# Float32 first tokens on two more queues, 128-token groups, spare PSUM banks for tile 0 and a new order search in a fused attention and MoE kernel

## The chip, the cores and the metric

The kernel runs on one core of a Trainium2 chip. The metric is the device time of one execution in microseconds (us). The profile's span, from the first to the last recorded instruction, is shorter: nearly every run shows 1.8 to 2.0 us between them (313.2 and 311.2 us, for example); two runs of pads0 show 2.8 and 3.2 us. All runs compared are of the state "fast" unless said otherwise.

Engines, as this kernel uses them: PE multiplies matrices, ACT and DVE work on vectors, POOL issues DMA with type conversion, SP issues DMA. Every engine has its own list of instructions, and in the traces here a blocked instruction holds up those behind it: in before, evictions on ACT stand 4.59 us behind an output DMA (shown below).

## The reference, cut to what matters

```python
# q, k, v: [8 batches, 8 heads, 576 tokens, 64], float32
scores = q @ k.T / 8, masked to |i - j| <= 32;  attn = softmax(scores);  o = attn @ v
x = o.transpose(0, 2, 1, 3).reshape(4608, 512)         # tokens x model
h = x @ w_in;  g = max(h, 0)**2;  out = g @ w_out      # w_in 512 x 2048, w_out 2048 x 512
```

## The kernel before

Attention is cut into 72 *steps* of 64 tokens (nine for each batch), the MoE into nine *tiles* of 512 tokens, so tile 0 is steps 0 to 7. For a step, K and Q are turned (transposed) on PE for batches 0 and 1 and by DMA later; then come scores, exp on ACT, mask on DVE, P V on PE, scaling on DVE, and a turn of the result into `XT`. A tile's first layer (`mm1`) reads `XT` and `w_in`; its second (`mm2`) reads `GT` and `w_out`. Tiles 0 and 1 run the first layer in *blocks*: 128 tokens by a quarter of `w_in`, 16 matmuls of 128 columns. Tile 0 has sixteen such blocks, and sixteen second-layer blocks of four matmuls of 512 columns.

```python
ORDER = ("k00 q00 v00 k01 q01 v01 k02 q02 v02 w10 w11 k03 q03 v03 w12 w13 k04 q04 v04 w20 w21 w22 w23 "
         "k10 q10 v10 ...").split()                      # order of the loads on POOL; w1x is w_in, w2x is w_out
PIECE = ((0, 96), (96, 128), (224, 128), (352, 128), (480, 96))    # first token, tokens

# PSUM: 8 banks of 128 x 512 float32
self.SC = ps("sc", [128, 2048], F32)                     # banks A C B D: scores A C, P V on B, turns on D
self.HT = [ps(f"ht{i}", [128, 512], F32) for i in range(2)]      # first layer
self.OUTP = [ps(f"outp{i}", [128, 512], F32) for i in range(2)]  # second layer

m = 1 if b < FB and not c else 2 if b < FB else 3        # steps in a group: 0 | 1 2 | 3 4 | 5 6 | 7 8
...
gt, op = self.GT[T % 2], self.OUTP[x % 2]                # mm2: two output banks
```

The program does not fix the order of the engines' instructions by hand. At build time it records operations with their dependencies, simulates them with assumed durations and DMA landings, and searches for a good order. Where PE has nothing to do in that simulation of the start, it puts *dummy matmuls* on zeros (line 398), which are meant to keep the clock up.

```python
for margin in MARGINS:                                   # 0, 4000, 10000, 20000 ns
    start, T = f[0], f[3]
    for k in range(ROUNDS):                              # 6
        R = self.backward(start, T)
        kk = [... r - (margin if op.att else 0) ...]     # priorities for the next forward pass
        start, end, out, T = self.forward(key=kk)
        keep(out, start, end, T, (margin, k))            # judged under 3 random draws of late DMA
```

The softmax here doesn't subtract the row's maximum and nothing guards it: scores larger than these inputs give would overflow.

## Time and profile before

| what | value |
|---|---|
| time, median of the first runs | 321.35 us (320.57 to 321.36) |
| span of the profiled run, its time | 321.0 us, 322.87 us |
| PE busy | 305.3 us, 95% |
| useful matmul time | 285.9 us |
| lost before 27 us, 27 to 75, 75 to 300, at the end | 18.4, 11.9, 1.6, 3.3 us |

"Useful" and "lost" are my sums and not lines of the profile. I count each real matmul with the spacing at which such matmuls follow each other in the chain of waits (0.216 us for 512 columns, 0.056 for 128, 0.031 for 65, 0.021 for 64) and dummies with zero. Lost time up to a moment is that moment minus the useful time of the matmuls begun by then. The busy share hides this: dummies are busy too.

First, the page of before: span, busy time, and the slices (40 equal parts of the span, in tenths).

```profile
span 321.0 us, 7141 instructions
...
PE 305.3 (95%) x2855; PEld 166.6 (52%) x2855; DVE 151.1 (47%) x448; ACT 148.4 (46%) x263; POOL 107.5 (33%) x133
...
PE   6889989789999998999999999999999999999996
...
DMA  9999999999997999999999999999992221000022
...
L398 PE MATMUL outp<-zz 128*128 128x512 bf16 x51 | 15.6, 409 | 1.2 <-DVE zz L392 1.2
```

PE looks full and DMA is full until about 240 us. But 51 of the matmuls are dummies.

Next, the timeline of PE in before (start, duration, engine, line, operation, result and sources, count, and in brackets the idle time before and what ended it). Lines 623 and 666 are first and second layer, 442 turns of K and Q, 605 turns of step results.

```profile
35.63 1.06 PE L623 MATMUL ht<-xt,w 128*128 128x128 bf16 x16
36.52 5.34 PE L666 MATMUL outp<-w,gt 128*128 128x512 bf16 x24
41.70 0.34 PE L442 MATMUL sc<-identw,kraw 96*128 96x96 bf16 x4
...
42.92 0.40 PE L605 MATMUL sc<-identw,xr 128*128 128x128 bf16 x4 [0.72 <-DVE qt L453]
...
44.50 1.06 PE L623 MATMUL ht<-xt,w 128*128 128x128 bf16 x16
```

Step 7 is paired with step 8, the last of batch 0. Their results are turned only at 42.92 us, behind batch 1's K and Q (41.70). They had been ready for 6.4 us: DVE scaled the second of them from 36.05 to 36.47 us. But the program records the turn of the next group's K and Q first, on the same bank D, so the turn of the results waits until batch 1's K and Q have landed and been copied out. So the ninth first-layer block of tile 0 is at 35.63 us, the tenth only at 44.50.

The timeline of ACT in before shows the stop that follows, and the table of windows what the clock did (columns: window, its length, busy time of PE, PEld (weight loads), DVE, ACT, POOL with counts, granted clock, DMA share, GB/s; the share adds up the packets begun in the window, so it can exceed 1).

```profile
59.96 0.60 ACT L675 ACTIVATE oe<-outp 128x512 f32<-128x512 f32 x1 [0.95 <-PE outp L666]
60.58 4.45 ACTq L677 DMA_DIRECT2D out_dram<-oe  x1
65.14 0.60 ACT L629 ACTIVATE rt<-ht 128x512 bf16<-128x512 f32 x1 [4.59 <-issue]
```

```profile
60.00:65.60 5.60, 2.38 (x51) 2.05 (x48) 0.77 (x3) 1.01 (x2) 1.67 (x2) 1.00 1.80 150
65.60:69.00 3.40, 3.21 (x27) 2.66 (x28) 1.80 (x5) 2.69 (x6) 0.87 (x1) 0.50 1.72 83
```

The first output DMA occupies ACT's queue for 4.45 us. The first-layer results behind it are not evicted, and PE has 2.38 us of work in 5.6 us. Then the clock is granted at half for 3.4 us.

### The profile page before, as it was taken

The numbers are of one execution on the slowest core, as the hardware profiler recorded it, in microseconds if no ns is written. First come the engines' busy times: TensorE is split into PE (matmuls) and PEld (weight loads), VectorE is DVE, ScalarE is ACT, GpSimd is POOL, SyncE is SP. The second block draws the span as 40 slices with busy tenths as digits, with TensorE's granted clock in tenths as the row PEclk, the third lists the DMA queues.
The fourth block names the chain that finished last, engine by engine and source line by source line (L and its number), as shares of the span: only waits on it lengthen the run. The fifth ranks groups of instructions, "written<-read, shape, count | busy, mean of one in ns | idle before, by whom it ended". The sixth has DMA issues, their size and how long they took to land.

```text
span 321.0 us, 7141 instructions
## 1 busy us (share of the span) xinstructions
PE 305.3 (95%) x2855; PEld 166.6 (52%) x2855; DVE 151.1 (47%) x448; ACT 148.4 (46%) x263; POOL 107.5 (33%) x133
## 2 busy tenths in 40 slices
PE   6889989789999998999999999999999999999996
PEld 2455768667755554454454454445444444444442
DVE  5845448445655674454455345545545432222200
ACT  2334436364544665455545545545535544344411
POOL 8999295414302552243333343333320000000000
PEclk9999999979999999999999999999999999999999
DMA  9999999999997999999999999999992221000022
GB/s 63 157 189 194 191 154 155 137 142 150 141 214 77 124 141 192 135 106 158 149 117 121 149 134 158 117 123 140 150 127 59 58 86 39 33 35 33 34 84 82
DMA packets 165922, 38.89 MB, mean 121 GB/s; under 512 B 157184, under 2 KB 161280, under 8 KB 165888
## 3 DMA queue, kind: packets, MB, share of 16 engines
q0 software_dynamic: 116736, 18.36, 86.7%
q1 hardware_dynamic: 43968, 10.63, 23.4%
q10 hardware_dynamic: 5184, 9.44, 9.7%
q8 instruction: 23, 0.38, 0.5%
q14 instruction: 11, 0.09, 0.1%
HBM read 36.70 MB, written 9.44 MB: 144 GB/s over the span
## 4 chain that ended last, share of the span: by engine, by line
PE 80%; DMA 8%; POOL 7%; ACTq 1%; ACT 1%; DVE 1%; issue 1%; SPq 0%; POOLq 0%; DVEq 0%
PE outp L666 37%; PE ht L642 29%; DMA vx<-in_v_dram 6%; PE ht L623 6%; PE sc L529 3%; PE sc L571 2%; PE sc L572 2%; POOL kraw L429 2%; POOL qraw L429 2%; DMA qt<-qraw 2%; POOL vx L478 2%; ACTq L677 1%; POOL w L498 1%; POOL w L493 1%; DVE pt L552 0%
## 5 line engine op out<-in xcount | busy, mean ns | idle before, releaser
L666 PE MATMUL outp<-w,gt 128*128 128x512 bf16 x576 | 143.8, 380 | 0.0
L642 PE MATMUL ht<-xt,w 128*128 128x512 bf16 x448 | 113.9, 379 | 0.0
L648 ACT ACTIVATE rt<-ht 128x512 bf16<-128x512 f32 x112 | 66.7, 599 | 93.2 <-PE ht L642 86.1
L657 DVE TENSOR_TENSOR gt<-rt 128x512 bf16<-128x512 bf16 x144 | 60.3, 422 | 79.7 <-ACT rt L648 68.2
L666 PEld LDWEIGHTS outp<-w,gt 128*128 128x128 bf16 x576 | 53.5, 98 | 58.8 <-issue 0.6
L642 PEld LDWEIGHTS ht<-xt,w 128*128 128x128 bf16 x448 | 41.9, 98 | 46.7
L429 POOL DMA_DIRECT2D kraw<-in_k_dram x40 | 35.3, 882 | 48.1 <-PE ht L642 31.5
L429 POOL DMA_DIRECT2D qraw<-in_q_dram x40 | 35.2, 879 | 43.8 <-PE ht L642 14.6
L478 POOL DMA_DIRECT2D vx<-in_v_dram x40 | 34.9, 873 | 38.2 <-PE sc L572 11.0
L545 ACT ACTIVATE e<-sc 128x512 bf16<-128x512 f32 x72 | 38.2, 601 | 9.5 <-PE sc L529 9.5
L623 PE MATMUL ht<-xt,w 128*128 128x128 bf16 x512 | 33.9, 222 | 4.8 <-ACT rt L629 3.4
L552 DVE TENSOR_TENSOR pt<-e,mask 128x512 bf16<-128x512 bf16 x72 | 26.9, 420 | 18.4 <-ACT e L545 18.2
L623 PEld LDWEIGHTS ht<-xt,w 128*128 128x128 bf16 x512 | 30.2, 99 | 8.5 <-ACT rt L629 4.8
L675 ACT ACTIVATE oe<-outp 128x512 f32<-128x512 f32 x36 | 21.5, 598 | 26.2 <-PE outp L666 26.2
L488 DVE COPY vd<-vx 64x1056 bf16<-64x1056 bf16 (+1 forms) x36 | 17.4, 483 | 28.3 <-DMA vx<-in_v_dram 27.8
L585 DVE TENSOR_TENSOR xr<-sc,rs 128x256 bf16<-128x256 f32 x72 | 29.7, 420 | 1.8
L629 ACT ACTIVATE rt<-ht 128x512 bf16<-128x512 f32 x32 | 19.2, 599 | 24.3 <-PE ht L623 19.5
L583 DVE RECIPROCAL rs<-sc 128x4 f32<-128x4 f32 x72 | 12.8, 180 | 15.4 <-PE sc L572 14.2
L398 PE MATMUL outp<-zz 128*128 128x512 bf16 x51 | 15.6, 409 | 1.2 <-DVE zz L392 1.2
L571 PE MATMUL sc<-vx,pt 128*128 128x65 bf16 x160 | 15.0, 192 | 0.5 <-DVE pt L552 0.3
L572 PE MATMUL sc<-vx,pt 128*128 128x65 bf16 x160 | 15.1, 193 | 0.0
L529 PEld LDWEIGHTS sc<-qt,kt 64*128 64x128 bf16 x576 | 10.0, 95 | 9.8 <-issue 7.9
(38 smaller groups left out, 128.3 us busy)
## 6 DMA issues: line engine op xcount, KB each, us to landing
out_dram<-oe ACTq DMA_DIRECT2D x36, 256.0 KB, 3.3
kraw<-in_k_dram POOLq DMA_DIRECT2D x30, 128.0 KB, 5.1
qraw<-in_q_dram POOLq DMA_DIRECT2D x30, 128.0 KB, 5.9
vx<-in_v_dram POOLq DMA_DIRECT2D x24, 128.0 KB, 5.0
w<-in_moe_w_in_dram POOLq DMA_DIRECT2D x4, 512.0 KB, 10.3
w<-in_moe_w_out_dram POOLq DMA_DIRECT2D x4, 512.0 KB, 17.0
vx<-in_v_dram POOLq DMA_DIRECT2D x16, 96.0 KB, 4.4
kt<-kraw SPq DMA_TRANSPOSE x30, 4.7
```

Of the source, the lines that this page charges most:

```text
L429: self.p.rec("POOL", lambda e: e.dma_start(dst, src), writes=[("fraw", b, t, x)], old=[("fraw", b - 2, t, x)], reads=self.pace(b, x, "kqv" ...
L478: self.p.rec("POOL", lambda e: e.dma_start(self.VX[b % 2][r:r + n, s, :, 0:64], self.v[b, :, t0:t0 + n, :].rearrange("h p d -> p h d")), w ...
L545: self.p.rec("ACT", lambda e, d=dst, a=src: e.activation(d, a, ACTF.Exp, scale=0.125), reads=["s" + x for x in name], writes=[("e", g, x) ...
L552: self.p.rec("DVE", lambda e, a=pt, c=ee, d=mb: e.tensor_tensor(a, c, d, ALU.mult), reads=rd + ["mask"], writes=[("pt", (n + k) % 3)], key ...
L572: mm = e.matmul(o, pt[:, a + 64:a + 192], vt[:, ha + 2, 0:VE], start=False, stop=True)
L585: self.p.rec("DVE", lambda e: e.tensor_tensor(bass.AP(xr, 256 * k, [[768, 128], [64, 4], [1, 64]]), bass.AP(self.SC, base, [[2048, 128], [ ...
L623: mm = e.matmul(ht[:, 128 * (d % 4):128 * (d % 4) + 128], self.W1[:, ft, 128 * d:128 * d + 128], self.XT[:, t0 // 64:t0 // 64 + 2, ft, :], ...
L642: mm = e.matmul(ht[:], self.W1[:, ft, 128 * d:128 * d + 128], self.XT[:, 8 * T:8 * T + 8, ft, :], start=(ft == 0), stop=(ft == 3))
L648: self.p.rec("ACT", lambda e: e.activation(rt[:], ht[:], ACTF.Relu), reads=[("ht", k % 2)], writes=[("rt", k % 4)], key=key, dur=560)
L657: self.p.rec("DVE", lambda e: e.tensor_tensor(g, r, r, ALU.mult), reads=[("rt", k % 4)], writes=tags, key=key, dur=430)
L666: mm = e.matmul(op[:], gt[:, d, 128 * u:128 * u + 128], self.W2[:, d, :], start=(d == 0), stop=(d == 15))
L675: self.p.rec("ACT", lambda e: e.activation(oe[:], op[:], ACTF.Copy), reads=[("outp", x % 2)], writes=[("oe", x % 4)], key=key, dur=560)
```

## The change: its intent and the diff

The change wants PE to start real work earlier and never to wait for batch 1 while work of tile 0 is left. It has five parts: (1) the first 96 tokens of Q, K, V come in float32 through the SP and ACT queues; (2) groups and pieces are aligned to 128 tokens, with 544 tokens early, so that tile 0 needs nothing of step 8; (3) P V of batch 0 alternates between two banks, the turns of its first steps use the first output bank, and the second layer of tile 0 also uses banks B and D; (4) `PACE` is 15 instead of 18, so later loads wait for later work; (5) the search also tries simulations in which every DMA lands later by a fixed amount.

```diff
-PACE = 18
+PACE = 15
-MARGINS, ROUNDS, NREP = (0, 4000, 10000, 20000), 6, 3
+PADS, MARGINS, ROUNDS, NREP = (0, 1000, 2000, 4000), (0, 4000, 10000), 3, 3
-ORDER = ("k00 q00 v00 k01 q01 v01 k02 q02 v02 w10 w11 k03 q03 v03 w12 w13 k04 q04 v04 w20 w21 w22 w23 "
+ORDER = ("k01 q01 v01 k02 q02 v02 w10 k03 q03 v03 w11 w12 k04 q04 v04 w13 w20 w21 w22 w23 k05 q05 "
+TURN0 = {1: 1, 2: 2, 4: 3, 6: 4}
+PIECE0 = ((0, 96), (96, 64), (160, 128), (288, 128), (416, 128), (544, 32))
@@ forward
-  end[op.i] = max(now, start[op.i] + op.dur) + POST[op.eng] + (rnd.random() * rnd.late[op.eng] if rnd else 0)
+  end[op.i] = max(now, start[op.i] + op.dur) + POST[op.eng] + (rnd.random() * rnd.late[op.eng] if rnd else pad)
@@ schedule
+        for pad in PADS:
+            f = self.forward(key=key, pad=pad)
+            for margin in MARGINS:
+                ...
+                    start, end, out, T = self.forward(key=kk, pad=pad)
@@ first loads (float32, no conversion)
+        self.p.rec(eng, lambda e: e.dma_start(dst, src), writes=[("oe", "kqv".index(t))], dma=(f"s{t}", 0), ...)
+                    self.first_load("k", "SP", -300)
+                    self.first_load("q", "ACT", -300)
+                    self.first_load("v", "SP", -299)
@@ banks
-        bank = "ACB"[k] if b >= FB else "B"
+        bank = "ACB"[k] if b >= FB else "BD"[n % 2] if n < 8 else "B"
+        trp, tag = (self.TRP, "sD") if n >= 8 else (self.OUTP[0][:].bitcast(BF16), ("outp", 0))
+        if x in (2, 3):                                  # second layer of tile 0
+            tag = "sB" if x == 2 else "sD"
+            op = self.BK[tag[1]]
@@ groups
-                m = 1 if b < FB and not c else 2 if b < FB else 3
+                m = 3 if b >= FB else 1 if not c or n in (1, 8) else 2
... (float32 turns and copies, keys of the second layer of tile 0, old= bookkeeping)
```

More of the change, by code (lines that the diff above doesn't have):

```diff
@@ L27 @@
 FB = 2
-PACE = 18
+PACE = 15
 ENGS = ("PE", "ACT", "DVE", "POOL", "SP")
-MARGINS, ROUNDS, NREP = (0, 4000, 10000, 20000), 6, 3
+PADS, MARGINS, ROUNDS, NREP = (0, 1000, 2000, 4000), (0, 4000, 10000), 3, 3
 LATE = {"POOL": 1500, "SP": 2000, "ACT": 2000}
 DEPTH, POST, BACK = 4000, {"POOL": 1500, "SP": 1000, "ACT": 1000}, {"POOL": 2500, "SP": 4000, "ACT": 4000}
-ORDER = ("k00 q00 v00 k01 q01 v01 k02 q02 v02 w10 w11 k03 q03 v03 w12 w13 k04 q04 v04 w20 w21 w22 w23 "
+ORDER = ("k01 q01 v01 k02 q02 v02 w10 k03 q03 v03 w11 w12 k04 q04 v04 w13 w20 w21 w22 w23 k05 q05 "
          "k10 q10 v10 k11 q11 v11 k12 q12 v12 k13 q13 v13 k14 q14 v14").split()
+GT0, WT0 = (12.5, 16, 19, 24), (13, 18, 21, 26)
+TURN0 = {1: 1, 2: 2, 4: 3, 6: 4}
+PIECE0 = ((0, 96), (96, 64), (160, 128), (288, 128), (416, 128), (544, 32))
 PIECE = ((0, 96), (96, 128), (224, 128), (352, 128), (480, 96))
@@ L92, in link, with forward @@
                 op.pred.append((d, hard))
-    def forward(self, key=None, seq=None, rnd=None):
+    def forward(self, key=None, seq=None, rnd=None, pad=0):
         ops = self.ops
@@ L282, in keep @@
                 best = (s, out, start, end, T)
-        f = self.forward(key=key)
-        keep(f[2], f[0], f[1], f[3], "keys")
-        for margin in MARGINS:
-            start, T = f[0], f[3]
-            for k in range(ROUNDS):
-                R = self.backward(start, T)
-                kk = [1e4 * op.key if op.key <= -100 else r - (margin if op.att else 0) for r, op in zip(R, self.ops)]
-                start, end, out, T = self.forward(key=kk)
-                keep(out, start, end, T, (margin, k))
+        for pad in PADS:
+            f = self.forward(key=key, pad=pad)
+            keep(f[2], f[0], f[1], f[3], ("keys", pad))
+            for margin in MARGINS:
+                start, T = f[0], f[3]
+                for k in range(ROUNDS):
+                    R = self.backward(start, T)
+                    kk = [1e4 * op.key if op.key <= -100 else r - (margin if op.att else 0) for r, op in zip(R, self.ops)]
+                    start, end, out, T = self.forward(key=kk, pad=pad)
+                    keep(out, start, end, T, (pad, margin, k))
         self.log, self.R = log, R
-        s, out, start, end, T = best
+        out = best[1]
+        start, end, out, T = self.forward(seq={e: [o for o in out if o.eng == e] for e in ENGS})
         for op in self.ops:
@@ L388, in alloc @@
         self.OE = [sb(f"oe{i}", [128, 512], F32) for i in range(4)]
+        self.STG = dict(zip("kqv", self.OE))
+        self.IDF = self.OE[3][:, 0:128]
     def ms(self, eng, t, ap, v, key, dur=120, old=()):
@@ L402, in setup_masks @@
                    key=key, dur=400)
+        self.p.rec("DVE", lambda e: e.tensor_scalar(self.IDF, self.IOTA[:, 0:128], 0.0, None, ALU.is_equal),
+                   reads=["iota"], writes=[("oe", 3)], key=key - 0.1, dur=200)
         self.p.rec("DVE", lambda e: e.tensor_scalar(self.IDW[:], self.IOTA[:], 64.0, None, ALU.is_equal),
@@ L423, in setup_ptz, with pieces, slot, first_load @@
             self.ms("DVE", [("ptz", i)], self.PT[i][:, 192 * j + 64:192 * j + 128], 0.0, key, 70)
+    def pieces(self, b):
+        return PIECE2 if b >= FB else PIECE if b else PIECE0
+    def slot(self, b, x):
+        return 512 * (x if b else x - 1)
+    def first_load(self, t, eng, key):
+        src = (self.q if t == "q" else self.k if t == "k" else self.v)[0, :, 0:96, :].rearrange("h p d -> p h d")
+        r = 32 if t == "v" else 0
+        dst = bass.AP(self.STG[t], 512 * r, [[512, 96], [64, 8], [1, 64]])
+        self.p.rec(eng, lambda e: e.dma_start(dst, src), writes=[("oe", "kqv".index(t))], dma=(f"s{t}", 0), key=key, dur=400,
+                   move=(48, 14))
@@ L425, in tok_load, with first_v @@
+    def first_v(self, key):
+        for r, n in ((32, 32), (64, 64)):
+            src = bass.AP(self.STG["v"], 512 * r, [[512, n], [64, 8], [1, 64]])
+            self.p.rec("ACT", lambda e, r=r, n=n, c=src: e.activation(self.VX[0][r:r + n, 0, :, 0:64], c, ACTF.Copy),
+                       reads=[("oe", 2)], writes=[("vxl", 0, 0) if r == 32 else ("vxl", 0, 0, 1)], key=key, dur=560, att=True)
     def tok_load(self, b, t, x, key):
-        t0, n = (PIECE if b < FB else PIECE2)[x]
+        t0, n = self.pieces(b)[x]
@@ L427, in tok_load @@
         src = (self.q if t == "q" else self.k)[b, :, t0:t0 + n, :].rearrange("h p d -> p h d")
-        dst = bass.AP(self.RAW[t][b % 2], 512 * x, [[2560, n], [64, 8], [1, 64]])
-        self.p.rec("POOL", lambda e: e.dma_start(dst, src), writes=[("fraw", b, t, x)], old=[("fraw", b - 2, t, x)],
-                   reads=self.pace(b, x, "kqv".index(t)), dma=(f"f{b % 2}{t}{x}", b), key=key,
+        dst = bass.AP(self.RAW[t][b % 2], self.slot(b, x), [[2560, n], [64, 8], [1, 64]])
+        y = x - 1 if not b else x
@@ L431, in tok_load @@
+        self.p.rec("POOL", lambda e: e.dma_start(dst, src), writes=[("fraw", b, t, x)], old=[("fraw", b - 2, t, y + (b == 2))],
+                   reads=self.pace(b, x, "kqv".index(t)), dma=(f"f{b % 2}{t}{y}", b), key=key,
                    dur=500 + 3.2 * n, move=(n // 2, 13.3))
     def tok_turn(self, b, x, key):
-        t0, n = PIECE[x]
+        t0, n = self.pieces(b)[x]
         early = b == 0 and x < 3
-        parts = [("k", ("ht", 0), self.HT[0][:].bitcast(BF16)), ("q", ("ht", 1), self.HT[1][:].bitcast(BF16))] if early else [
-            ("k", "sD", self.TRP[:, 0:512]), ("q", "sD", self.TRP[:, 512:1024])]
+        first = b == 0 and x == 0
@@ L439, in f @@
+        if early:
+            parts = [(t, ("ht", u), self.HT[u][:] if first else self.HT[u][:].bitcast(BF16)) for u, t in enumerate("kq")]
+        elif b or x == 5:
+            parts = [("k", "sD", self.TRP[:, 0:512]), ("q", "sD", self.TRP[:, 512:1024])]
+        else:
+            o = self.OUTP[0][:].bitcast(BF16)
+            parts = [("k", ("outp", 0), o[:, 0:512]), ("q", ("outp", 0), o[:, 512:1024])]
         def f(e, todo):
@@ L441, in f @@
                 for j in range(4):
-                    mm = e.transpose(ps[:, 128 * j:128 * j + n],
-                                     bass.AP(self.RAW[t][b % 2], 512 * x + 128 * j, [[2560, n], [1, 128]]),
-                                     self.ID[0:n, 0:n])
+                    src = bass.AP(self.STG[t], 128 * j, [[512, n], [1, 128]]) if first else bass.AP(
+                        self.RAW[t][b % 2], self.slot(b, x) + 128 * j, [[2560, n], [1, 128]])
+                    mm = e.transpose(ps[:, 128 * j:128 * j + n], src, self.IDF[0:n, 0:n] if first else self.ID[0:n, 0:n])
             return mm
         for todo in ([parts[:1], parts[1:]] if early else [parts]):
-            self.p.rec("PE", lambda e, a=todo: f(e, a), reads=[("fraw", b, t, x) for t, _, _ in todo] + ["id"],
-                       writes=list({tag for _, tag, _ in todo}), key=key, dur=240 * len(todo), att=True)
+            rd = [("oe", "kq".index(t)) for t, _, _ in todo] + [("oe", 3)] if first else [("fraw", b, t, x) for t, _, _ in todo]
+            self.p.rec("PE", lambda e, a=todo: f(e, a), reads=rd + ["id"],
+                       writes=list({tag for _, tag, _ in todo}), key=key, dur=700 if first else 240 * len(todo), att=True)
         for t, tag, ps in parts:
@@ L452, in tok_turn @@
             dst = self.KT[b % 2][:, :, 32 + t0:32 + t0 + n] if t == "k" else self.QT[b % 2][:, :, t0:t0 + n]
-            self.p.rec("DVE", lambda e, d=dst, c=src: e.tensor_copy(d, c), reads=[tag], writes=[(t, b % 2, x)],
-                       old=self.was(b, t, x), key=key, dur=400, att=True)
+            if early and t == "q":
+                self.p.rec("ACT", lambda e, d=dst, c=src: e.activation(d, c, ACTF.Copy), reads=[tag], writes=[(t, b % 2, x)],
+                           old=self.was(b, t, x), key=key, dur=200 + 2.8 * n, att=True)
+            else:
+                self.p.rec("DVE", lambda e, d=dst, c=src: e.tensor_copy(d, c), reads=[tag], writes=[(t, b % 2, x)],
+                           old=self.was(b, t, x), key=key, dur=60 + 3.2 * n, att=True)
     def pace(self, b, x, z):
@@ L464, in was @@
             return []
-        return [(t, b % 2, y) for y in range(5)]
+        return [(t, b % 2, y) for y in range(6)]
     def dma_turn(self, b, t, x, key):
@@ L479, in vx_load @@
             self.VX[b % 2][r:r + n, s, :, 0:64], self.v[b, :, t0:t0 + n, :].rearrange("h p d -> p h d")),
-            writes=[("vxl", b % 2, s)], reads=self.pace(b, s, 2), dma=(f"vf{b % 2}{s}", b), key=key, dur=500 + 3.2 * n, move=(n // 2, 13.3))
+            writes=[("vxl", b % 2, s), ("vxl", b % 2, s, 1)], reads=self.pace(b, s, 2), dma=(f"vf{b % 2}{s}", b), key=key, dur=500 + 3.2 * n, move=(n // 2, 13.3))
     def vd_half(self, b, s0, s1, key):
@@ L486, in vd_half @@
             src = vx[64 - 64 * lo:128 - 64 * lo, s0 + lo:s1 + lo, :, :].rearrange("p s h d -> p (s h d)")
-            rd = [("vxl", b % 2, s + lo) for s in range(s0, s1)] + [("vxone", b % 2, k) for k in range(4)]
+            rd = [("vxl", b % 2, s + lo) + u for s in range(s0, s1) for u in ((), (1,))] + [("vxone", b % 2, k) for k in range(4)]
             self.p.rec("DVE", lambda e, d=dst, c=src: e.tensor_copy(d, c), reads=rd,
@@ L504, in qk_tags @@
         rd = [("ktpad", i, 0), ("ktpad", i, 1)]
-        for x, (t0, n) in enumerate(PIECE if b < FB else PIECE2):
+        for x, (t0, n) in enumerate(self.pieces(b)):
             if t0 < 64 * c + 96:
@@ L575, in av @@
         if c % 2 == 0:
-            rd = [("vxl", i, s)] + [("vxone", i, k) for k in range(4)]
+            rd = [("vxl", i, s), ("vxl", i, s, 1)] + [("vxone", i, k) for k in range(4)]
             if s in (0, 4):
@@ L604, in f @@
                     o = 256 * u + 128 * t
-                    mm = e.transpose(self.TRP[:, o:o + 128], xr[:, u, 128 * t:128 * t + 128], self.ID)
+                    mm = e.transpose(trp[:, o:o + 128], xr[:, u, 128 * t:128 * t + 128], self.ID)
             return mm
-        self.p.rec("PE", f, reads=[("xr", gi % 3, u) for u in range(m)] + ["id"], writes=["sD"], key=key, dur=112 * m, att=True)
-        src = self.TRP[:, 0:256 * m].rearrange("p (n f q) -> p n f q", n=m, f=4)
+        self.p.rec("PE", f, reads=[("xr", gi % 3, u) for u in range(m)] + ["id"], writes=[tag], key=key, dur=112 * m, att=True)
+        src = trp[:, 0:256 * m].rearrange("p (n f q) -> p n f q", n=m, f=4)
         self.p.rec("ACT", lambda e: e.activation(self.XT[:, n:n + m], src, ACTF.Copy),
-                   reads=["sD"], writes=[("xt", n + u) for u in range(m)], key=key, dur=200 + 180 * m, att=True)
+                   reads=[tag], writes=[("xt", n + u) for u in range(m)], key=key, dur=200 + 180 * m, att=True)
     def mm1_small(self, T, g, q, key):
@@ L661, in mm2 @@
         x = 4 * T + u
-        gt, op = self.GT[T % 2], self.OUTP[x % 2]
+        gt, op, tag = self.GT[T % 2], self.OUTP[x % 2][:], ("outp", x % 2)
+        if x in (2, 3):
+            tag = "sB" if x == 2 else "sD"
+            op = self.BK[tag[1]]
         def f(e):
             for d in range(4 * seg, 4 * seg + 4):
-                mm = e.matmul(op[:], gt[:, d, 128 * u:128 * u + 128], self.W2[:, d, :], start=(d == 0), stop=(d == 15))
+                mm = e.matmul(op, gt[:, d, 128 * u:128 * u + 128], self.W2[:, d, :], start=(d == 0), stop=(d == 15))
             return mm
         self.p.rec("PE", f, reads=[("gt", T % 2, d, u) for d in range(4 * seg, 4 * seg + 4)] + [("w2", seg)],
-                   writes=[("outp", x % 2)], key=key, dur=854)
+                   writes=[tag], key=key, dur=854)
         if x == 1 and seg == 0:
@@ L674, in mm2 @@
             oe = self.OE[x % 4]
-            self.p.rec("ACT", lambda e: e.activation(oe[:], op[:], ACTF.Copy), reads=[("outp", x % 2)],
+            self.p.rec("ACT", lambda e: e.activation(oe[:], op, ACTF.Copy), reads=[tag],
                        writes=[("oe", x % 4)], key=key, dur=560)
@@ L681, in moe @@
         if T == 0:
-            gt = (12.0, 15.5, 19.0, 22.0)
-            wt = (13.0, 18.0, 22.0, 28.0)
-            for g, q in sorted(((g, q) for g in range(4) for q in range(4)), key=lambda a: (max(gt[a[0]], wt[a[1]]), a)):
-                self.mm1_small(0, g, q, 0.0 + 0.01 * self.k1)
+            for g, q in sorted(((g, q) for g in range(4) for q in range(4)), key=lambda a: (max(GT0[a[0]], WT0[a[1]]), a)):
+                self.mm1_small(0, g, q, 0.01 * self.k1)
+            for seg in range(4):
+                for u in range(4):
+                    self.mm2(0, u, seg, 0.5 + seg + 0.1 * u)
             return
@@ L692, in moe @@
                 self.mm1(T, d, key)
-            self.mm2(T - 1, d // 4, d % 4, key + 0.25)
+            if T > 1:
+                self.mm2(T - 1, d // 4, d % 4, key + 0.25)
     def build(self):
@@ L701, in build @@
         self.setup_idle()
-        self.setup_masks(K + 2.5)
+        self.setup_masks(K - 20)
         self.setup_rest(0, K + 3)
@@ L718, in build @@
             if b < FB:
-                for bb in range(FB if not b else 0):
-                    for x in range(5):
-                        for t in "kq":
-                            self.tok_load(bb, t, x, at[f"{t}{bb}{x}"])
-                        self.vx_load(bb, x, at[f"v{bb}{x}"])
+                if not b:
+                    self.first_load("k", "SP", -300)
+                    self.first_load("q", "ACT", -300)
+                    self.first_load("v", "SP", -299)
+                    self.first_v(-LEAD - 2.5)
+                for bb in range(0 if b else FB):
+                    for x in range(6):
+                        for t in "kqv":
+                            if f"{t}{bb}{x}" not in at:
+                                continue
+                            if t == "v":
+                                self.vx_load(bb, x, at[f"v{bb}{x}"])
+                            else:
+                                self.tok_load(bb, t, x, at[f"{t}{bb}{x}"])
             else:
@@ L736, in build @@
                         self.tok_turn(0, 0, -LEAD - 3)
+                    if n == 8:
+                        self.moe(0)
+                        tile = 1
+                        self.tok_turn(0, 5, -LEAD + 5)
                     self.scores(n, m)
@@ L739, in build @@
                         bb, cc = divmod(n + m, NCH)
-                        self.tok_turn(bb, (cc + 1) // 2, n + m - LEAD - 3)
+                        if n + m != 8:
+                            self.tok_turn(bb, (cc + 1) // 2 if bb else TURN0[cc], n + m - LEAD - 3)
+                if c and not b:
                     x = (c + 1) // 2
-                    if x and not b:
+                    if c % 2:
                         self.vd_half(b, x - 1, x, n - LEAD - 3)
```

## The prediction

> **What bounds the kernel now.** PE, 95% busy on the page; the chain of waits is 80% PE. But the first slices hold dummy matmuls (51 on zeros) and waits. I add up useful matmuls at their spacing in the chain (four of 512 columns 0.86 us, sixteen of 128 columns 0.89 us; dummies zero). Useful work is about 286 us of the 321.0 us span, so 35 us are lost: 19 before 27 us, 11 from 27 to 75 us, 1.5 from there to 300 us, 3 at the end. Only the start-up can shrink; PE work hardly changes.
>
> **Start-up, from DMA landings and the PE timeline.** Transfers land one after the other: 128 tokens of one tensor each 0.83 us, a weight quarter each 2.6 us; w_in quarters at 16.8, 19.5, 24.5, 27.1 us, w_out at 31.5 to 40.4, batch 1 complete at 51.7 us. The first K lands at 4.4 us: POOL starts issuing at 1.3 us, 0.9 us each. Steps 6 and 7 are turned in pairs (5,6), (7,8); step 7 only at 42.9 us, behind batch 1's K and Q. So PE has done nine of tile 0's sixteen first-layer blocks at 36.5 us, does six second-layer blocks, waits for batch 1, and finishes the sixteen near 53 us; ten second-layer blocks remain after 58 us. At 60.6 us the first output DMA holds the ACT queue 4.45 us, PE stops 3.4 us behind it, and the granted clock is 0.79 from 64 to 72 us.
>
> **What the change does.**
> - Three pieces of 96 tokens leave POOL (2.5 us of issue) for the SP and ACT queues. They must stay float32: the Trainium skill, "DMA: Bandwidth & Descriptors", section "SWDGE vs HWDGE vs iDMA", says only the software queue casts; in the trace POOL issues all casting loads. Float32 turns and ACT copies cost about 3 us on idle engines. The bytes stay; the stream comes 1.5 to 2.5 us earlier (estimate).
> - Groups aligned to 128 tokens, 544 tokens loaded early: steps 6,7 are ready near 28 us, not 43. The sixteen blocks end near 33 us instead of 53.
> - Two more output banks and separate keys: sixteen second-layer blocks (13.8 us) fit into 33 to 48 us, while batch 1 lands. Tile 1 follows without a gap.
> - A smaller PACE holds later loads back by six first-layer blocks, partly cancelling the earlier PE.
>
> **Sum.** Lost before 27 us: 13.4 instead of 19 (nine blocks of 0.89 us and seven steps of attention are useful by then). From 27 to 75 us: 3 to 5 instead of 11. Ideal about 306 us. I give back 4 us: DMA engines read 9 tenths up to 240 us, and from 113 to 124 us PE already waits on a Q transpose; PE 12 us earlier meets batches 2 to 4 with less lead. The early outputs also issue from ACT while DMA is full.
>
> **Predicted: 310.5 us, range 303.5 to 318.5; faster by over 2% 0.78, within 2% 0.20, slower 0.02.**
>
> **What the profile would show.** Right: first K turned by 4.4 us; w_in's first quarter landed near 14 us; tile 0's first layer done before 35 us, its second by 50 us; clock 1.0 from 60 to 75 us; batch 1 complete near 49.5 us; 22 us lost by 75 us instead of 30. Wrong: a step of tile 0 turned after 35 us, PE gaps over 1 us from 30 to 75 us, ACT queue issues over 2 us.
>
> **What would make it wrong.** The instruction orders come from a simulated schedule; a wrong landing in it stops in-order PE. Three queues share the same engines, so the float32 pieces could delay POOL's. Batches 2 and 3 may come too late, giving back up to 8 us near 80 to 125 us.

## The result, and the profile after

After takes 313.18 us (median of 4 runs, 312.09 to 313.32); before took 320.96 us in the same rounds. The ratio is 0.9754, 95% interval 0.9722 to 0.9787. Ratios here and below are the mean time of one kernel's fast runs over that of the other's of the same rounds, so they are not quite the ratio of the medians that I quote. A second set, on another chip, gave 0.9751.

The lines of the page of after that answer to those of before:

```profile
span 311.2 us, 7131 instructions
...
PE 302.4 (97%) x2850; PEld 166.0 (53%) x2850; DVE 147.3 (47%) x448; ACT 151.5 (49%) x269; POOL 105.8 (34%) x132
...
PE   5999999999999999999999999999999999999996
...
DMA  9999999999979999999899999999999220000021
```

The dummies are down to 38. The timeline of PE in after (line 665 first layer, 711 second layer, 479 turns of K and Q, 647 turns of step results):

```profile
22.00 1.07 PE L665 MATMUL ht<-xt,w 128*128 128x128 bf16 x16
22.91 0.81 PE L405 MATMUL outp<-zz 128*128 128x512 bf16 x3
23.56 0.39 PE L479 MATMUL outp<-identw,kraw 128*128 128x128 bf16 x4
...
25.53 0.40 PE L647 MATMUL outp<-identw,xr 128*128 128x128 bf16 x4 [0.29 <-DVE qt L493]
...
26.62 1.96 PE L665 MATMUL ht<-xt,w 128*128 128x128 bf16 x32
...
31.55 0.39 PE L647 MATMUL outp<-identw,xr 128*128 128x128 bf16 x4
...
40.65 1.06 PE L665 MATMUL ht<-xt,w 128*128 128x128 bf16 x16
41.54 2.75 PE L711 MATMUL sc<-w,gt 128*128 128x512 bf16 x12
```

Steps 6 and 7 are turned at 31.55 us, 11 us earlier than step 7 was. The sixteenth first-layer block starts at 40.65 us, and second-layer work on the spare banks (`sc<-w,gt`) fills the rest. The ACT timeline and the windows of after show the stop gone:

```profile
42.60 0.60 ACT L720 ACTIVATE oe<-sc 128x512 f32<-128x512 f32 x1 [0.27 <-PE sc L711]
43.23 0.36 ACTq L722 DMA_DIRECT2D out_dram<-oe  x1
```

```profile
60.00:65.60 5.60, 4.83 (x72) 3.88 (x72) 3.55 (x13) 1.79 (x3) 1.23 (x2) 1.00 1.80 175
65.60:69.00 3.40, 3.40 (x65) 2.89 (x63) 2.11 (x7) 3.10 (x6) 1.58 (x3) 1.00 1.38 194
```

Landings of loads, read from the trace, in us:

| load | before | after |
|---|---|---|
| first K | 4.39 | 4.14 |
| w_in quarters | 16.81, 19.53, 24.45, 27.05 | 12.64, 19.23, 21.25, 26.14 |
| last w_out quarter | 40.40 | 36.30 |
| batch 1 complete | 51.70 | 48.95 |

Lost time as defined above, by part of the run, in us:

| | to 27 us | 27 to 75 | 75 to 300 | end | all |
|---|---|---|---|---|---|
| before | 18.4 | 11.9 | 1.6 | 3.3 | 35.1 |
| after | 17.7 | 1.8 | 2.7 | 3.2 | 25.4 |
| predicted for after | 13.4 | 3 to 5 | about 5.5 | 3 | about 26 |

Nearly all of the gain comes from 27 to 75 us. The profiled run of before was 1.5 us slower than the median of its other runs, so the spans differ by 9.8 us and the times by 7.8.

### The profile page after: what moved, and what is told of

Same layout as the page of the kernel before. It is cut to its first block, busy times and chain, and to the rows that moved or that the text cites. A ratio compares the mean times of both kernels' runs of the same rounds, so it can differ in the third digit from the quotient of the medians.

```text
span 311.2 us, 7131 instructions
## 1 busy us (share of the span) xinstructions
PE 302.4 (97%) x2850; PEld 166.0 (53%) x2850; DVE 147.3 (47%) x448; ACT 151.5 (49%) x269; POOL 105.8 (34%) x132
## 4 chain that ended last, share of the span: by engine, by line
PE 82%; DMA 12%; issue 2%; DVE 1%; ACT 1%; POOL 1%; SPq 0%; POOLq 0%; ACTq 0%
PE outp L711 33%; PE ht L684 27%; PE ht L665 8%; DMA vx<-in_v_dram 7%; PE sc L569 3%; PE sc L611 3%; PE sc L612 2%; PE outp L405 2%; DMA kraw<-in_k_dram 2%; DMA kt<-kraw 2%; DMA oe<-in_v_dram 1%; PE sc L711 1%; DVE vd L528 1%; PE outp L647 0%; POOL qraw L458 0%
## 5 line engine op out<-in xcount | busy, mean ns | idle before, releaser
L711 PE MATMUL outp<-w,gt 128*128 128x512 bf16 x544 | 132.3, 379 | 0.0
L684 PE MATMUL ht<-xt,w 128*128 128x512 bf16 x448 | 109.6, 379 | 0.0
L711 PEld LDWEIGHTS outp<-w,gt 128*128 128x128 bf16 x544 | 51.1, 98 | 57.8
L684 PEld LDWEIGHTS ht<-xt,w 128*128 128x128 bf16 x448 | 42.0, 98 | 47.7 <-ACT rt L690 0.5
L458 POOL DMA_DIRECT2D qraw<-in_q_dram x40 | 33.8, 846 | 48.3 <-PE ht L684 21.8
L458 POOL DMA_DIRECT2D kraw<-in_k_dram x40 | 33.9, 848 | 46.0 <-PE ht L684 21.7
L518 POOL DMA_DIRECT2D vx<-in_v_dram x39 | 33.2, 852 | 34.1 <-PE ht L684 25.5
L720 ACT ACTIVATE oe<-outp 128x512 f32<-128x512 f32 x34 | 20.4, 599 | 27.2 <-PE outp L711 27.2
L665 PE MATMUL ht<-xt,w 128*128 128x128 bf16 x512 | 31.9, 219 | 0.2
L665 PEld LDWEIGHTS ht<-xt,w 128*128 128x128 bf16 x512 | 29.1, 98 | 2.2 <-ACT xt L652 0.7
L569 PE MATMUL sc<-qt,kt 64*128 64x64 bf16 x576 | 13.7, 192 | 0.5 <-ACT qt L490 0.3
## 6 DMA issues: line engine op xcount, KB each, us to landing
w<-in_moe_w_out_dram POOLq DMA_DIRECT2D x4, 512.0 KB, 16.7
```

The costliest lines, as they stand in the source:

```text
L458: self.p.rec("POOL", lambda e: e.dma_start(dst, src), writes=[("fraw", b, t, x)], old=[("fraw", b - 2, t, y + (b == 2))], reads=self.pace( ...
L518: self.p.rec("POOL", lambda e: e.dma_start(self.VX[b % 2][r:r + n, s, :, 0:64], self.v[b, :, t0:t0 + n, :].rearrange("h p d -> p h d")), w ...
L569: mm = e.matmul(sc[:, o + 64 * j:o + 64 * j + 64], kt[r, j, at:at + 128], qt[r, j, at:at + 64], start=True, stop=True)
L665: mm = e.matmul(ht[:, 128 * (d % 4):128 * (d % 4) + 128], self.W1[:, ft, 128 * d:128 * d + 128], self.XT[:, t0 // 64:t0 // 64 + 2, ft, :], ...
L684: mm = e.matmul(ht[:], self.W1[:, ft, 128 * d:128 * d + 128], self.XT[:, 8 * T:8 * T + 8, ft, :], start=(ft == 0), stop=(ft == 3))
L711: mm = e.matmul(op, gt[:, d, 128 * u:128 * u + 128], self.W2[:, d, :], start=(d == 0), stop=(d == 15))
```

## The experiments

**Theory A:** the gain is made of several parts, each worth some us: the earlier load stream, the groups, the spare banks. **Rival B:** the earlier stream alone is the cause. **Rival C:** the new order search alone is the cause. Each run below undoes one part of after, or puts one part alone on before. Such an edit also makes the search find another order for the whole program, so what a run differs by is that part *with* the order found for it. An order alone can move the time of the same program by 1.5 us (pad3000 against after) or 10 us (pads0), so a difference of 3 or 4 us is put down to a part only as far as the trace shows where it arises.

| run | edit | median us | ratio to before (95%) |
|---|---|---|---|
| after | | 313.18 | 0.9754 (0.9722 to 0.9787) |
| after_again | none, another chip | 312.9 | 0.9751 (0.9726 to 0.9776) |
| before_again | none | 321.79 | 1.001 (0.9963 to 1.0057) |
| pool_first | after, first tokens by POOL | 317.0 | 0.9873 (0.9818 to 0.9927) |
| groups_old | after, groups of before | 317.13 | 0.9878 (0.9822 to 0.9934) |
| mm2_two | after, two output banks | 316.48 | 0.986 (0.979 to 0.993) |
| pv_b | after, P V and result turns as before | 316.38 | 0.9847 (0.9825 to 0.9868) |
| turn_ht | after, K and Q turns on other banks | 315.46 | 0.9825 (0.9788 to 0.9863) |
| pads0 | after, search of before | 323.24 (322.81 without a slow run) | 1.0045 (1.0009 to 1.0081) |
| b_search | before, search of after | 321.11 | 1.0007 (0.9958 to 1.0057) |
| pace18 | after, PACE 18 | 314.17 | 0.9775 (0.9723 to 0.9827) |
| pad3000 | after, search with 3 us alone | 311.64 | 0.9702 (0.9666 to 0.9739) |
| turn4_d_3000 | pad3000 and one turn on bank D | 314.28 | 0.975 (0.9711 to 0.9788) |

Nine of the traces from these rounds (before_again, after_again, pool_first, groups_old, mm2_two, turn_ht, pads0, turn4_d_3000 and pv_b) lack 1 to 2% of the matmul records; the eight kernels of the after family among them have 2,796 to 2,818 of about 2,850. A missing record would count as lost time, so for these I give lost time only up to 50 us, and read later parts from waits and clock.

### before_again (no edit)

> The kernel before, unchanged, profiled once more: a control. Theory: the first profile of before (time 322.87 us, span 321.0) caught an exceptional stop of the ACT queue (4.45 us at its first output, PE stopped 3.4 us behind it, clock halved for 3.4 us); the timed runs of before lie 1.5 us lower. So here: time near 321, span near 319.2, no ACT queue issue over 2 us, mean granted clock 1.0. Rival: the stop is regular, and shows again with about the same length. Ratio to before 1.000 either way.

Measured: time 322.56 us in the profiled run, span 320.7. The ACT queue is held again, for 4.23 us at 60.19 us, and the clock is halved for 6.8 us from 64.0 us. My theory falls and the rival holds: the stop is regular. All but one of the eleven runs of before in these rounds have mean granted clocks of 0.988 to 0.995; one or two stretches of 3.4 us at half clock give that. The gap between span and time, 1.8 to 2.0 us, is there in every run of this round.

### pool_first

```diff
-ORDER = ("k01 q01 ...
+ORDER = ("k00 q00 v00 k01 q01 ...
-        first = b == 0 and x == 0
+        first = False                    # bf16 pieces by POOL; the float32 loads are taken out
```

> The kernel after, but the first 96 tokens of Q, K, V are loaded by POOL with the cast to bfloat16, as before; groups, banks and search stay. Theory A (the groups and the banks carry most of the gain, the earlier stream 2 to 3 us): 315 to 316 us, first-layer weights landing 1.5 to 3 us later than in after. Rival B (the earlier stream carries nearly all of it): 319 us or more. Rival C (the float32 path gives nothing, since DMA is saturated from the start): 313 us.

Measured: 317.0 us, ratio 0.9873. The w_in quarters land at 15.52, 21.82, 24.03 and 28.90 us (after: 12.64, 19.23, 21.25, 26.14) and batch 1 is complete at 51.73 us instead of 48.95. Lost time at 27 us is 18.6 us instead of 17.7, at 50 us 21.0 instead of 18.1. So the earlier stream is worth 2.6 to 2.9 us of landing and about 0.012 of the ratio, a little more than theory A said. Rival C's reading (nothing) is refuted. Rival B's (nearly all) does not fit the median, though the interval just reaches its 319 us (0.991).

### groups_old

```diff
-PIECE0 = ((0, 96), (96, 64), (160, 128), (288, 128), (416, 128), (544, 32))
+PIECE0 = ((0, 96), (96, 128), (224, 128), (352, 128), (480, 96))
-                m = 3 if b >= FB else 1 if not c or n in (1, 8) else 2
+                m = 3 if b >= FB else 1 if not c else 2
                 # and the turns, moe(0) and k05 q05 as before
```

> The kernel after, but with the step groups, token pieces and turn order of before (pairs 1-2, 3-4, 5-6, 7-8; no 544-token piece); float32 start, banks and search stay. Theory A: step 7 is turned only behind batch 1's keys, the sixteen first-layer blocks of tile 0 end after 45 us again, and the time goes back to 316 to 319 us. Rival B (the earlier stream is the cause): within 1 us of after, 312 to 314 us.

Measured: 317.13 us, ratio 0.9878. The sixteenth first-layer block of tile 0 starts at 47.9 us (after: 40.65). Up to 30 us this run has lost even less than after (16.7 against 17.7 us), but 5.7 us more are lost from there to 50 us, against 0.4 in after. As theory A said: the old pairs cost their time between 30 and 50 us, waiting for batch 1. The timeline of PE shows the waits (line 611 is P V of step 7, on bank D behind batch 1's K and Q; line 647 the turn of its result):

```profile
37.37 0.33 PE L479 MATMUL sc<-identw,kraw 96*128 96x96 bf16 x4 [0.96 <-DMA qraw<-in_q_dram]
...
38.59 0.20 PE L611 MATMUL sc<-vd,pt 128*128 128x65 bf16 x1 [0.72 <-DVE qt L493]
...
39.74 0.40 PE L647 MATMUL outp<-identw,xr 128*128 128x128 bf16 x4 [0.52 <-DVE xr L625]
40.83 8.08 PE L665 MATMUL ht<-xt,w 128*128 128x128 bf16 x112 [0.69 <-ACT xt L652]
```

The four stops are 2.9 us together, and the clock is halved for 3.4 us from 41.2 us, which is up to 1.7 us more.

### mm2_two

```diff
-        if x in (2, 3):
+        if False:
-            for seg in range(4):
-                for u in range(4):
+            for u in range(4):
+                for seg in range(4):      # two banks: a row block must be closed before the next opens
```

> The kernel after, but the second layer of tile 0 uses the two output banks alone (row blocks one after the other instead of four at once); all else stays. Theory A: second-layer blocks of tile 0 must wait for whole row blocks of the first layer and for evictions, so a part of the gain goes: 314.5 to 317 us. Rival (banks do not matter, since PE always finds other work in 27 to 60 us): within 1 us of after.

Measured: 316.48 us (315.35 to 319.53, a wide spread), ratio 0.986. By 50 us PE has begun ten second-layer blocks instead of twelve (counted by their weight loads, since matmul records are missing), and one wait of 2.8 us for a scaled step result follows, with the clock halved for 3.4 us from 61.0 us:

```profile
61.72 0.61 PE L647 MATMUL sc<-identw,xr 128*128 128x128 bf16 x4 [2.77 <-DVE xr L625]
```

The time is in the size theory A gave. That the two banks cause this wait, and not the order found with them, is not shown.

The three parts together (0.012, 0.012 and 0.011 of the ratio) are more than the whole gain of 0.025. They are not independent: each removes stops, and a stop also costs clock. The mean granted clock shows it: 0.988 to 0.995 in all four runs of groups_old and 0.989 to 0.995 in three of the four of mm2_two, as in before, against 0.998 to 1.0 in after and 0.999 to 1.0 in pool_first.

### after_again, pads0 and b_search: the search

After_again is a control on the chip of pads0.

> The kernel after, unchanged: a control on this chip beside the other variants. Ratio to before 0.974 to 0.977, so 312.5 to 314.5 us if before is near 321.5; all times 1.8 to 2.0 us above their spans, as in every run so far.

Measured: 312.9 us, ratio 0.9751, as expected.

```diff
# pads0: after, with the search of before
-PADS, MARGINS, ROUNDS, NREP = (0, 1000, 2000, 4000), (0, 4000, 10000), 3, 3
+PADS, MARGINS, ROUNDS, NREP = (0,), (0, 4000, 10000, 20000), 6, 3
```

> The kernel after with the schedule search of before (no added DMA delay in the search; four margins, six rounds). If the new search is a cause of its own (a rival to groups, banks and stream), the time goes back by 2 us or more, 315 us and up; if not, within 1 us of after.

Measured: 323.24 us with one slow run, 322.81 us without, ratio 1.0045: *the whole gain is gone*. (Two of the runs have an unusually large gap of 2.8 and 3.2 us between span and time; by spans alone, 319.8 to 320.5 us, there is still no gain.) Up to 50 us the run is like after_again (both have lost about 18.9 us). The loss comes later. The waits of PE in pads0 from 75 to 300 us (total, times, longest), and the longest of them in its timeline:

```profile
PE sc L569 <- DMA qt<-qraw: 4.2, 4, 2.7
PE ht L684 <- DMA xt<-xr: 2.2, 2, 1.7
```

```profile
158.72 0.54 PE L569 MATMUL sc<-qt,kt 64*128 64x64 bf16 x24 [2.73 <-DMA qt<-qraw]
```

PE stands in front of scores whose turned Q has not landed, although further down its list stands work that then starts without a wait of its own (a first-layer block at 159.18 us). The clock is halved for 3.4 us from 159.1 us. In the windows from 100 to 200 us PE is busy 46.10 and 46.29 of 50 us each in pads0, against 49.83 and 49.44 in after, and 49.37 and 49.53 in after_again, whose trace lacks as many records. In after, the waits listed for PE from 20 to 300 us hold only 0.2 us for DMA.

```diff
# b_search: before, with nothing of the change but the search
-MARGINS, ROUNDS, NREP = (0, 4000, 10000, 20000), 6, 3
+PADS, MARGINS, ROUNDS, NREP = (0, 1000, 2000, 4000), (0, 4000, 10000), 3, 3
                 # forward(pad=...) and the loop over PADS as in the diff of the change
```

> The kernel before with nothing of the change but the new search of the instruction orders (each candidate also searched with 0, 1, 2 or 4 us added to every DMA landing). Theory (the search and the shorter start-up only pay together: the search removes stops that appear when PE runs ahead of DMA, and before has hardly any, 1.5 us from 75 to 300 us): 319 to 322 us, ratio 0.992 to 1.003. Rival (the search is the gain by itself, and start-up adds nothing, as the run without it, 323.2 us, could also be read): 313 to 315 us.

Measured: 321.11 us, ratio 1.0007. The search alone gives nothing. So the new start without the new search is worth nothing, the new search without the new start is worth nothing, and both together are worth 2.5%. The margins and rounds of pads0 include those of after, so what its search lacks is the added delay. One order was built for each search, so how much of the 10 us is the delay and how much the luck of that one order is not separated. Rival C falls as "alone" and stays as "necessary".

### pv_b and turn_ht: the shared bank

In after the turn of steps 4 and 5 (25.53 us above) uses the same bank as the last full turn of K and Q (23.56 us), and waits for its copies, although the scaled result was ready at 23.0 us.

```diff
# pv_b: P V of batch 0 on B alone, turns of results on D
-        bank = "ACB"[k] if b >= FB else "BD"[n % 2] if n < 8 else "B"
+        bank = "ACB"[k] if b >= FB else "B"
-        trp, tag = (self.TRP, "sD") if n >= 8 else (self.OUTP[0][:].bitcast(BF16), ("outp", 0))
+        trp, tag = (self.TRP, "sD")
```

> The kernel after, but P V of batch 0 on bank B alone and the turns of its results on bank D, as before; the turns of K and Q stay on the first output bank. Theory: in after the turn of steps 4,5 waits 2.5 us (ready at 23.0, run at 25.5 us) because it shares the bank with the turn of the last K and Q piece; with banks of their own it runs by 23.5 us and one to three first-layer blocks move before 26 us: 0 to 2 us faster than after, 311 to 314 us. Rival (the second P V bank is what matters): P V of a pair is serialized by its scaling, and the time is 0.5 to 2 us longer than after.

Measured: 316.38 us, ratio 0.9847. The time is on the rival's side and longer than it said. The profiled run fell in a slow state (523.75 us at a granted clock of 0.566), so its trace cannot say why; the four fast runs agree within 0.3 us.

```diff
# turn_ht: pieces 3 and 4 of K and Q are turned on the first-layer banks
-        early = b == 0 and x < 3
+        early = b == 0 and x < 5
```

> The kernel after, but pieces 3 and 4 of K and Q are turned on the two first-layer banks, as pieces 0 to 2 are, so that the turn of steps 4,5 shares no bank with them. Theory: the turn of steps 4,5 comes earlier, but first-layer blocks wait for these banks instead; within 1.5 us of after, either way. Rival (the shared bank costs all of the 3.6 us that I missed before 27 us): 310.5 us or less.

Measured: 315.46 us, ratio 0.9825. First-layer work is pushed back as feared: the first block starts at 23.4 us (after: 14.4), and lost time at 27 us is 18.5 us. The cost is larger than the 1.5 us expected.

### pace18

```diff
-PACE = 15
+PACE = 18
```

> The kernel after with PACE 18 again: loads of batches 2 on may go out six first-layer blocks earlier. My prediction's term: the smaller PACE holds loads back and gives a little of the gain back. Then earlier loads help in 80 to 130 us: 311.5 to 313 us. Rival (early loads of batch 2 crowd the start-up, where DMA is full, so batch 1 or the weights land later): 314 to 317 us, with batch 1 complete later than 49.5 us.

Measured: 314.17 us, ratio 0.9775. The interval overlaps nearly all of that of after, so PACE decides nothing that I can see. The time lies in the rival's range, but its mark does not show: batch 1 is complete at 48.37 us, not later than 49.5. My prediction's term, that the smaller PACE gives a part of the gain back, is not supported.

### pad3000

```diff
-PADS, MARGINS, ROUNDS, NREP = (0, 1000, 2000, 4000), (0, 4000, 10000), 3, 3
+PADS, MARGINS, ROUNDS, NREP = (3000,), (0, 4000, 10000), 3, 3
```

> The kernel after with the search run at one added DMA delay of 3 us (after's order came from the candidate with 2 us). Theory: in-order waits on late DMA are what is left between 75 and 300 us (2.7 us in after, 10 us and more in the run without added delay), so more reserve removes 0.5 to 2 us: 311 to 313 us, no PE wait on DMA after 75 us. Rival (2 us is enough, and more reserve displaces other work): 313 to 316 us.

Measured: 311.64 us (310.91 to 312.84, 6 runs), ratio 0.9702. It beats before clearly and has the lowest time and profiled span (309.8 us) of all runs. Against after's two sets its interval overlaps (0.9666 to 0.9739 against 0.9726 to 0.9776), so that it beats after is likely, not shown. Its trace is complete: 1.1 us are lost from 75 to 300 us instead of 2.7, the start to 50 us is as in after, and no wait of PE for DMA is left after 20 us. That is the theory's half of the expectation.

### turn4_d_3000

```diff
# pad3000, and:
-        elif b or x == 5:
+        elif b or x >= 4:                 # piece 4 of K and Q is turned on bank D ...
-                        if n + m != 8:
+                        if n + m not in (6, 8):
                 self.av(n)
+                if n == 5:                # ... recorded after P V of step 5
+                    self.tok_turn(0, 4, 6 - LEAD - 3)
```

> The run with 3 us of added delay (0.970 of before), and one thing more: the last full piece of K and Q is turned on bank D, recorded after P V of step 5, so that the turn of steps 4,5 neither shares its bank nor waits behind it. Theory (this shared bank explains most of the 3.6 us by which I overrated the gain before 27 us): the turn of steps 4,5 runs by 23.7 us instead of 25.5, lost PE time at 30 us falls from 17.6 to under 16 us, and the time is 0.5 to 2 us lower, 309.5 to 311 us. Rival (as the two earlier runs with other banks suggest, blocks moved forward are paid back by steps 6,7, whose turn on D waits longer, and by bank D being taken): lost time at 30 us over 17, time 312 to 315 us.

Measured: 314.28 us, ratio 0.975. Its timeline of PE:

```profile
22.82 1.07 PE L665 MATMUL ht<-xt,w 128*128 128x128 bf16 x16
23.73 0.39 PE L647 MATMUL outp<-identw,xr 128*128 128x128 bf16 x4
...
93.07 0.20 PE L611 MATMUL sc<-vx,pt 128*128 128x65 bf16 x1 [1.73 <-DVE pt L592]
...
95.14 0.82 PE L569 MATMUL sc<-qt,kt 64*128 64x64 bf16 x24 [0.98 <-DVE xr L625]
```

The turn of steps 4 and 5 does move, from 25.51 us in pad3000 to 23.73. It saves little: lost time at 27 us is 16.6 instead of 17.6 us, at 30 us 17.0 instead of 17.6. So neither expectation holds whole: 17.0 lies above the theory's 16, and the time is the rival's. What the new order costs comes later. At 93 us PE stops twice, 2.7 us together, and the windows around it show what the clock made of that:

```profile
84.00:91.00 7.00, 6.84 (x85) 3.58 (x86) 3.65 (x12) 2.08 (x5) 0.00 (x0) 1.00 0.59 127
91.00:94.40 3.40, 1.43 (x48) 1.11 (x40) 1.73 (x8) 2.05 (x4) 0.00 (x0) 0.98 0.52 135
94.40:101.20 6.80, 6.06 (x44) 2.89 (x45) 3.23 (x10) 2.77 (x5) 1.75 (x2) 0.51 0.46 51
101.20:108.00 6.80, 6.75 (x46) 3.24 (x45) 3.50 (x10) 3.77 (x7) 3.98 (x5) 1.00 1.32 98
```

Half a clock over 6.8 us is another 3.4 us at most, on top of 2.7. The runs of this kernel with a full clock (313.48 and 313.82 us) are still 2 us slower than pad3000; where these 2 us go is open, since the trace lacks records.

## Why the prediction was right or wrong, point by point

The time was within the range (310.5 predicted, 303.5 to 318.5; measured 313.2), and faster by over 2% was the likely side. The mechanism was right where the gain arose, from 27 to 75 us. That the sum of the losses came so near (26 us predicted, 25.4 measured) is partly luck: 4.3 us too little before 27 us were balanced by about 2 us too much from 27 to 75 us and about 3 us too much after that.

- **Time against span: wrong by 1.9 us.** I worked from the span of one profiled run (321.0 us) and set its result beside a time (321.35 us) as if they were one thing. They only looked alike because that run was itself 1.5 us slow: its time was 322.87 us. Its own terms also add up to more than I wrote: 321.0 minus 5.6 minus about 7 is 308, not "ideal about 306"; with 4 given back, 312 us of span. Measured: 311.2.
- **"Lost before 27 us: 13.4 instead of 19": the step that was mis-sized most.** Measured 17.7 in after, against 18.4. I took nine first-layer blocks to be done by then; four were begun before 26.6 us (14.41, two at 19.37, 22.00). I had counted a step as ready a few us after its data landed. In fact the last V piece of steps 4 and 5 landed at 15.19 us and the results were turned at 25.53. In turn4_d_3000, without the shared bank (and with another order), the turn comes 1.8 us earlier and 1.1 us less is lost at 27 us; I take the rest to be the chain of scores, exp, mask, P V and scaling on engines in order, which I did not take apart. I also overlooked the clock of the first microseconds. Its record begins, at full, only at 11.62 us in after (4.18 in before, 9.38 in before_again), and the page's PEclk row shows nothing of this; but dummies of 512 columns follow each other at about twice the distance until then:

```profile
7.43 1.89 PE L405 MATMUL outp<-zz 128*128 128x512 bf16 x4
...
13.54 1.02 PE L405 MATMUL outp<-zz 128*128 128x512 bf16 x4
```

By my spacings 1.7 us of useful work in after was begun before 11.62 us (in before none before 4.18), so up to 1.7 us (my estimate) of the 4.3 us that I missed may be the clock.

- **"From 27 to 75 us: 3 to 5 instead of 11": the direction right, and the gain larger.** Measured 1.8 instead of 11.9. Groups_old, mm2_two and pool_first each lose a part of it. The finer claims failed: the first layer of tile 0 ended near 41.5 us and not before 35, and the second at about 60 us (the fourth output eviction of tile 0 is at 60.05 us) and not by 50. It did not matter, since PE had first-layer blocks of tile 1 in between.
- **"The stream comes 1.5 to 2.5 us earlier": slightly small.** Measured 2.8 us for batch 1 (51.70 to 48.95), and pool_first takes it back. "W_in's first quarter near 14 us": 12.64.
- **"I give back 4 us" from batches 2 to 4: too much for this kernel, about 1.1 us (1.6 to 2.7), and for a reason I missed.** The danger was real: pads0 gives back everything. I read the diff's loop over added delays as a detail and named the simulated schedule only as a risk. It is the part that keeps the gain.
- **Clock 1.0 from 60 to 75 us, no PE gap over 1 us from 30 to 75, no ACT queue issue over 2 us, no tile 0 step turned after 35 us, 22 us lost by 75 us (19.5): right** (longest PE gap 0.77 us at 60.78 us, longest ACT output issue in 40 to 75 us 0.36 us). I treated the ACT stop as a cost of 3.4 us and did not count the clock separately, which is 1.7 us for each 3.4 us at half.
- **PACE "partly cancelling": not supported** (pace18).

What stays open: why the output DMA holds ACT's queue for over 4 us at 60 us in before and 0.36 us in after. Pool_first, groups_old and mm2_two have no such stop either (0.34 to 0.40 us), so no single one of their parts is needed to remove it; I have no run that isolates its cause. The traces hold one lead. Of all output issues on ACT in 13 traces (all but pv_b's), the 463 at which at most four of SP's DMA transposes were under way, issued and not landed, took 0.40 us at most. All three that were held (before, before_again and b_search, 4.1 to 4.5 us) fell where five were under way. But two others with five (groups_old at 54.09 us, mm2_two at 56.83 us) took 0.35 and 0.40 us, so this is a lead and not a cause.

## What to carry to other kernels

When a change makes the busiest engine run ahead at the start, search the fixed orders again with reserve for landings: here the gain was otherwise given back as waits in front of DMA a hundred us later. Test the order apart from the change. Count useful work, not busy time, when a kernel fills gaps with dummies. A stop of a few us on PE can cost as much again through the clock (2.7 us of stops were followed by 6.8 us at half clock), so remove stops before shaving work.

## What the Trainium skill lacked or had wrong

- "DMA: Bandwidth & Descriptors", section "Issuing engines are not separate DMA queues", says that issuing from several engines only saves the issuing sequencer's time, usually small. The trace agrees with the first half: POOL spent 0.89, 0.78 and 0.81 us on the three first pieces, 2.5 us together, and moving them brought batch 1 in 2.8 us earlier. It was not small here: POOL needs about 0.88 us to issue a piece of 128 tokens that then takes 0.83 us to land behind the one before.
- "TensorE: Matmul & The Clock Gate", section "What's actually happening", ties the halved clock to an idle window of about 3.4 us. The stretches at half clock here are indeed 3.4 or 6.8 us. But a window that was not idle was enough: in turn4_d_3000 PE was busy 1.59 of the 3.41 us before the clock fell (90.84 to 94.25 us), its longest stop 1.73 us. The page does not say how much work keeps the clock up. Cut into windows of 3.41 us that end where the clock fell, the 13 traces show seven falls before the end of the program, each after a window with 0.17 to 1.59 us of PE busy; once the clock was full, it stayed full after every window with 1.64 us or more. Some of these traces lack 1 to 2% of the matmul records, so the border is rough.
- "Perfetto Trace Analysis", section "Identifying the Most-Contended Engine", says that matmul busy share is a poor measure and names weight-load share and the share of peak arithmetic. The first half is right here (95% busy with 35 of 321 us lost). Weight-load share hardly helps either: 52% before, 53% after, as dummies load weights too.
- No page that I read treats a program whose engine orders are fixed at build time. What reserve for DMA landings was worth here, each with the one order found: 322.8 us (fast runs) without added delay, 313.2 us where the search could use up to 4 us, 311.6 us with 3 us.
